# Fourteen of sixteen experts taken in order of token count, with a static row count for each place in the order

## The chip, the cores and the metric

The kernel runs on one core of a Trainium2 chip. The metric is device time in microseconds (us) of one launch, attention and mixture of experts together. The times in this document come from timed runs and from one profiled execution; stretches are given in us from the start of that execution's span.

## What is computed

A delta-rule attention over 768 steps (4 batches, 8 heads, head size 48) gives 3072 tokens of 384 features. A two-level gate then picks one of four groups and one of four experts in it for each token, and each token goes through its own expert alone: 384 to 1024 features, ReLU, and back to 384, times the two softmax weights.

```python
# x: (3072, 384), the attention's output, one row for each token
g_idx = np.argmax(x @ w_group, axis=1)
for g in range(4):
    mask_g = g_idx == g
    xg = x[mask_g]
    e_idx = np.argmax(xg @ w_expert[g], axis=1)
    for e in range(4):
        mask_e = e_idx == e
        h = np.maximum(xg[mask_e] @ w1[g, e], 0.0)
        ye = h @ w2[g, e]
        out[tok_idx] = (g_w * e_w)[:, None] * ye     # 0 for no token: each has one expert
```

How many tokens an expert gets depends on the data. For the inputs of this case (a fixed seed) the reference routes 203, 162, 176, 211, 203, 190, 203, 201, 181, 200, 183, 224, 195, 202, 155 and 183 tokens to experts 0 to 15. That is 3072 in all, 192 on average, and 224 at most.

## The kernel before

**Attention.** The tokens are worked through in 24 chunks of 32 steps. TensorE makes the products, VectorE inverts small triangular matrices (`inverse`), and ScalarE empties the accumulators. The order of these engines is written out by hand.

**Routing.** After each group of chunks `route` picks the expert of every token, and counts in `acc` how many tokens each expert has so far. Each expert owns a region of `room` rows in a DRAM buffer `x_dram`. A token's row number is the count before it (`slot_i`), and GpSimd writes the token there by an indirect DMA (L464), with its weight `cw` (L456, copied by L463) and its own number beside it. The regions' first 224 rows are zeroed at the start of the kernel (L177, 16 DMAs), so that rows with no token hold zeros. When all chunks are counted, a matmul with ones (L597) gives the totals of each expert, `last` (L598). From them L600 to L606 work out how many extra tiles of 128 tokens there are beyond the static 224 rows of each expert (`over`, its running sum `incl`, and the total `tot_i`).

**Experts.** The sixteen experts follow in their own order, 0 to 15, each with `SLOTS = 224` rows, in two halves of 112. TensorE, VectorE and ScalarE again run in the order in which the code is written; SyncE's queue, which issues the loads, is filled by the scheduler. For expert e:

- `take` (L616) reads its 224 rows from `x_dram` into `xg`, two experts ahead.
- `turn_in` (L625) transposes the rows, six transposes in all, and L627 copies them to `xt`.
- `hidden` (L636): 8 tiles of hidden features times 3 blocks of input features, each with a 128x128 block of `w1` as the stationary operand and the 224 rows as the moving one. Each product in 32-bit floats is two matmul records in the trace, so these are 48 records. ScalarE applies ReLU (L639).
- `second` (L650): 3 blocks of output features times 8 tiles, 48 records again. ScalarE copies (L652).
- `turn_out` (L661, L664, L665): six transposes, the product with the weight, and an indirect DMA from GpSimd that puts each row at its token's place in `out`. Rows with no token point beyond the end and are dropped.
- When `hidden` and `second` of expert e are done with their weights, the two buffers are reloaded with `w1` and `w2` of expert e + 2 (L122, 1536 KB each).

The halves of `turn_in` of the next expert lie between the parts of `second`, those of `turn_out` of the last expert between the parts of `hidden`. After the sixteen a loop of run-time length (L709) works through the extra tiles, `n_over` of them, one at a time. It reads the counts, loads the weights of that expert, takes 128 rows and sends them through the same steps with nothing beside it.

Of the kernel before, what the change touches and what calls it, by code (L numbers as in the profile page):

```python
# [8 lines left out]
F32 = mybir.dt.float32  # L9
I32 = mybir.dt.int32  # L10
# [8 lines left out]
SLOTS = 224  # L19
# [4 lines left out]
def constants(n_tokens, seq, n_experts, n_group, n_batch, room):  # L24
# [18 lines left out]
        "full": np.tile(first + SLOTS - 127, (128, 1)),  # L43
# [11 lines left out]
def deltanet_then_moe(  # L55
# [27 lines left out]
    T, P = 2, SLOTS // 2  # L83
    assert room % 32 == 0 and SLOTS % 32 == 0 and room >= N + 128
# [9 lines left out]
    x_dram = dp.tile([NE * room // 32, 32, XW], F32, name="x_dram")  # L94
# [7 lines left out]
    over = cp.tile([128, NE], F32, name="over")  # L102
    incl = cp.tile([128, NE], F32, name="incl")
# [11 lines left out]
    def load_expert(e, w1, w2, parts=1):  # L115
# [8 lines left out]
        return out  # L124

    weights = {}

    with ExitStack() as first:
# [31 lines left out]
        zero = ap_.tile([P, XW], F32, name="zero")  # L160
# [3 lines left out]
        def load_rest():  # L164
# [11 lines left out]
            for e in range(NE):  # L176
                nc.sync.dma_start(out=slots(e), in_=zero[:, None, :].to_broadcast([P, T, XW]))  # L177
# [196 lines left out]
        def route(r):  # L374
# [83 lines left out]
            for g, u in enumerate(us):  # L458
                x = xs.pop(u)
                if n == RG:  # L460
# [4 lines left out]
                    out=x_dram.rearrange("a b d -> (a b) d"),  # L465
# [132 lines left out]
        nc.vector.tensor_copy(last, n_ps)  # L598
        tiles_i = cp.tile([128, NE], I32, name="tiles_i")
        nc.vector.tensor_tensor(tiles_i, last, cut["full"], op=ALU.subtract)  # L600
# [74 lines left out]
    ready = {0: take(slots(0)), 1: take(slots(1))}  # L675
    xts, yts = {0: turned(ready[0][0])}, {}
    with tc.manual_schedule(engines={mybir.EngineType.PE, mybir.EngineType.DVE,
# [3 lines left out]
        for e in range(NE):  # L681
            if e + 2 < NE:
                ready[e + 2] = take(slots(e + 2))
# [25 lines left out]
    with tc.For_i(0, n_over):  # L709
        done = mp.tile([128, NE], F32, name="done")  # L710
# [6 lines left out]

        nc.vector.tensor_scalar(col, col, 4.0, float(SLOTS // 32), op0=ALU.mult, op1=ALU.add)
        nc.vector.scalar_tensor_tensor(col, in0=ef, scalar=float(room // 32), in1=col,
                                       op0=ALU.mult, op1=ALU.add)  # L720
# [8 lines left out]
                            max_val=NE * room // 32 - 4,  # L729
                            skip_runtime_bounds_check_because="a tile of the sorted tokens")  # L730
        end, lim = mp.tile([128, NE], F32, name="end"), mp.tile([128, 1], F32, name="lim")
        nc.vector.tensor_scalar(end, cut["expert"], ef, None, op0=ALU.is_equal)
# [72 lines left out]
```

## Time and profile before

| | us |
|---|---|
| median of 3 runs | 619.71 |
| lowest, highest | 618.38, 621.3 |
| the profiled execution, its own time | 617.58 |
| its span from the first to the last instruction | 615.8 |

| engine | busy us | share of the span |
|---|---|---|
| TensorE matmul (PE) | 517.1 | 84% |
| TensorE weight load (PEld) | 474.4 | 77% |
| VectorE (DVE) | 240.8 | 39% |
| ScalarE (ACT) | 175.7 | 29% |
| GpSimd (POOL) | 72.1 | 12% |

The shares are averages over two different stages, so they say little by themselves. Attention and routing end at about 280 us. The experts follow until about 601 us, and the last rows are written after that. A row of the trace names a line, an engine, an operation, the tiles that it writes and reads, its shapes and how often it ran. In a row of stages, the number after each engine is its busy time in that stretch; the granted clock is that of TensorE as a share of its full 2.4 GHz, so that 0.50 is 1.2 GHz.

### The profile page before, as it was taken

To read this page: it belongs to the slowest core of one execution; us is meant where nothing else is said; L and a number is where in the kernel's file an instruction comes from. 1 tells how busy PE (TensorE), PEld (TensorE's weight loads), DVE (VectorE), ACT (ScalarE), POOL (GpSimd) and SP (SyncE) were. 2 spreads that over 40 slices of the span, in tenths; PEclk is the share of its full clock that TensorE was granted. 3 is DMA by queue.
4 is the path that set the end of the run, shared out by engine and by line. 5 is a ranking of instruction groups with operands and counts; after the bars stand their busy time and mean duration, and the time that the engine had idled before them with its cause. 6 is when DMAs were issued, how large, how long until landed. Compare 5 with 4: busy or idle time off the path is not lost. (4 is left out here: it accounts for less than half of the span.)

```text
span 615.8 us, 18005 instructions
## 1 busy us (share of the span) xinstructions
PE 517.1 (84%) x8070; PEld 474.4 (77%) x8070; DVE 240.8 (39%) x738; ACT 175.7 (29%) x335; POOL 72.1 (12%) x130
## 2 busy tenths in 40 slices
PE   3305789979989788863999999999999999999990
PEld 2204667767767676752999999999999999999990
DVE  2698967989699894141011111011111111111000
ACT  2103245554655645430111111111111111111110
POOL 0100000003030132141011001110011000110011
PEclk9999679988979899985999999999999999999996
DMA  8996543425322132223255647555574655746000
GB/s 294 379 279 221 195 161 133 133 78 172 131 86 65 47 103 86 60 79 93 102 197 185 199 159 247 177 206 183 178 247 146 232 165 197 242 153 215 11 15 20
DMA packets 40351, 96.54 MB, mean 157 GB/s; under 512 B 3369, under 2 KB 24034, under 8 KB 40272
## 3 DMA queue, kind: packets, MB, share of 16 engines
q1 hardware_dynamic: 36688, 85.90, 42.2%
q0 software_dynamic: 3584, 9.47, 4.4%
q8 instruction: 64, 1.05, 0.7%
q14 instruction: 15, 0.12, 0.1%
HBM read 80.36 MB, written 15.78 MB: 156 GB/s over the span
## 5 line engine op out<-in xcount | busy, mean ns | idle before, releaser
L636 PE MATMUL h_ps<-xt,w 128*128 128x224 f32 x768 | 155.1, 356 | 0.6 <-DVE xt L627 0.6
L650 PE MATMUL y_ps<-hid,w 128*128 128x224 f32 x768 | 153.3, 353 | 0.0
L636 PEld LDWEIGHTS h_ps<-xt,w 128*128 128x128 f32 x768 | 144.7, 192 | 1.3 <-DVE xt L627 0.9
L650 PEld LDWEIGHTS y_ps<-hid,w 128*128 128x128 f32 x768 | 143.0, 190 | 0.0
L627 DVE COPY xt<-t_ps 128x336 f32<-128x336 f32 x32 | 16.2, 508 | 167.5 <-PE t_ps L625 167.5
L639 ACT ACTIVATE hid<-h_ps 128x448 f32<-128x448 f32 x64 | 34.8, 544 | 140.3 <-PE h_ps L636 140.3
L664 DVE TENSOR_SCALAR yo<-o_ps,xg 112x384 f32<-112x384 f32 x32 | 19.7, 617 | 120.4 <-PE o_ps L661 120.4
L665 POOL DMA_INDIRECT out_dram<-yo,at x32 | 30.1, 941 | 296.9 <-DVE yo L664 236.5
L264 DVE TENSOR_TENSOR m<-m,t 128x30 f32<-128x30 f32 (+9 forms) x180 | 59.5, 331 | 4.7
L260 DVE TENSOR_TENSOR t<-m 128x30 f32<-128x30 f32 (+9 forms) x180 | 59.4, 330 | 4.2
L297 PE MATMUL a_ps<-vh,con 128*128 128x384 f32 x48 | 26.9, 649 | 34.8 <-DVE vh L284 22.6
L652 ACT ACTIVATE yt<-y_ps 128x224 f32<-128x224 f32 x48 | 17.2, 357 | 134.3 <-PE y_ps L650 134.3
L335 ACT ACTIVATE s_bd<-s_ps 48x768 f32<-48x768 f32 x46 | 37.0, 804 | 17.3 <-PE s_ps L329 16.7
L297 PEld LDWEIGHTS a_ps<-vh,con 128*128 128x128 f32 x48 | 8.4, 218 | 37.8 <-DVE vh L284 19.8
L329 PE MATMUL s_ps<-w,kv 32*128 32x96 f32 x736 | 28.2, 292 | 4.7 <-ACT w L322 4.7
L303 PEld LDWEIGHTS a_ps<-s_bd,kqt 128*32 128x32 f32 x736 | 18.1, 125 | 15.9 <-issue 15.9
L319 PEld LDWEIGHTS w_ps<-f,mtb 64*64 64x64 f32 x768 | 25.4, 139 | 6.3 <-issue 4.0
L329 PEld LDWEIGHTS s_ps<-w,kv 32*128 32x128 f32 x736 | 24.3, 198 | 7.3 <-ACT w L322 5.7
L319 PE MATMUL w_ps<-f,mtb 64*64 64x48 f32 x768 | 28.4, 225 | 1.1 <-ACT f L307 1.1
L340 PE MATMUL o_ps<-w,gq 32*32 32x48 f32 x1536 | 24.2, 212 | 2.7 <-issue 2.7
L203 PE MATMUL g_ps<-kqt 48*32 48x64 f32 x1216 | 18.6, 249 | 7.8 <-DMA kqt<-in_kq_dram 4.1
L464 POOL DMA_INDIRECT x_dram<-x,slot_i x24 | 23.7, 986 | 8.7 <-POOL x L463 5.0
(95 smaller groups left out, 459.5 us busy)
## 6 DMA issues: line engine op xcount, KB each, us to landing
w<-in_w_dram SPq DMA_DIRECT2D x28, 1536.0 KB, 6.8
kqt<-in_kq_dram SPq DMA_DIRECT2D x24, 512.0 KB, 4.4
kv<-in_kv_dram SPq DMA_DIRECT2D x24, 448.0 KB, 3.9
x_dram<-zero SPq DMA_DIRECT2D x16, 337.8 KB, 9.4
xg<-x_dram SPq DMA_DIRECT2D x16, 337.8 KB, 3.2
w<-in_w_dram SPq DMA_DIRECT2D x6, 512.0 KB, 8.5
w<-in_w_dram SPq DMA_DIRECT2D x4, 576.0 KB, 7.7
w<-in_w_dram SPq DMA_DIRECT2D x2, 384.0 KB, 6.8
```

The lines of the kernel that those rows point to most:

```text
L260: nc.vector.tensor_tensor(tv, m[:, j + 1:, j:j + 1].to_broadcast([128, n, j]), m[:, j:j + 1, 0:j].to_broadcast([128, n, j]), op=ALU.mult)
L264: nc.vector.tensor_tensor(m[:, j + 1:, 0:j], m[:, j + 1:, 0:j], tv, op=ALU.add)
L297: nc.tensor.matmul(a_ps.rearrange("p h d -> p (h d)"), lhsT=ident, rhs=vh.rearrange("p h d -> p (h d)"), start=True, stop=(u == 0), skip_g ...
L319: nc.tensor.matmul(w_ps[b, h], lhsT=mt[b, uu * H + (h % 2) * NP + h // 2], rhs=f[b, h], start=True, stop=True, skip_group_check=True)
L329: nc.tensor.matmul(s_at[:, b, j], lhsT=k[quads[b], j], rhs=w[quads[b], 2 * j:2 * j + 2], start=(u == 0 and j == 0), stop=True, skip_group_ ...
L335: nc.scalar.activation(s_bd[rows, :, :, hh, :], s_at[rows, :, :, hh * D:(hh + 1) * D], ACT.Copy)
L340: nc.tensor.matmul(o_ps[b, h], lhsT=gq[b, (h % 2) * NP + h // 2], rhs=w[b, h], start=(u == 0 and h == 0), stop=True, skip_group_check=True)
L464: put = nc.gpsimd.indirect_dma_start(out=x_dram.rearrange("a b d -> (a b) d"), out_offset=bass.IndirectOffsetOnAxis(ap=slot_i[:, g], axis= ...
L636: nc.tensor.matmul(h_ps[:, k], lhsT=w1[:, j, (f + k) * 128:(f + k + 1) * 128], rhs=xt[:, j], start=(j == 0), stop=(j == DC - 1), skip_grou ...
L639: nc.scalar.activation(hid[:, f:f + 2], h_ps, ACT.Relu)
L650: nc.tensor.matmul(y_ps, lhsT=w2[:, f, j * 128:(j + 1) * 128], rhs=hid[:, f], start=(f == 0), stop=(f == FC - 1))
L665: nc.gpsimd.indirect_dma_start(out=out[:, :], out_offset=bass.IndirectOffsetOnAxis(ap=at[:, i:i + 1], axis=0), in_=yo[:, :], in_offset=Non ...
```

## The change

The experts 0 and 1 (`FIXED = 2`) stay first, with 224 static rows each. The other fourteen are sorted by their token count, the largest first, on the chip, once the totals are known. Place k of that order has its own static number of rows: 232, 220, 214, 208, 204, 202, 200, 196, 192, 188, 184, 182, 176 and 168. The loop over sixteen experts is then a loop over places, and which expert stands at a place is read from the table `order_i` into a register of SyncE (L718 of the changed kernel), which addresses the rows in `x_dram` and the two weight matrices. `slots_of` keeps for each expert the static rows that it got, for the count of extra tiles and for the loop over them.

The sort makes a 16x16 table of comparisons, sums it into a rank, compares the rank with 0 to 15, and sums twice more, for `order` and for `slots_of`. The tables are 256 elements wide on each partition. The constants grow by 32 columns, and the zeroed part of each region from 224 to 232 rows. In the loop over extra tiles the row arithmetic is in rows and no longer in blocks of 32; it is left out of the diff here.

```diff
-SLOTS = 224
+FIXED = 2
+SLOTS = [224] * FIXED + [232, 220, 214, 208, 204, 202, 200, 196, 192, 188, 184, 182, 176, 168]
...
-    def slots(e):
-        rows = x_dram[e * room // 32:(e * room + SLOTS) // 32].rearrange("a b d -> (a b) d")
-        return rows.rearrange("(p t) d -> p t d", t=T)
+    def slots(e, n):
+        return x_dram[e, 0:n].rearrange("(o p t) d -> p (o t) d", o=1, t=T)
...
+    def load_any(ev, w1, w2):
+        for t, d in ((w1, w1_d), (w2, w2_d)):
+            nc.sync.dma_start(out=t, in_=d[ds(ev, 1)].rearrange("o (c p) f -> p (o c) f", p=128))
...
-                nc.sync.dma_start(out=slots(e), in_=zero[:, None, :].to_broadcast([P, T, XW]))
+                nc.sync.dma_start(out=slots(e, max(SLOTS)),
+                                  in_=zero[:, None, :].to_broadcast([max(SLOTS) // T, T, XW]))
...
         nc.vector.tensor_copy(last, n_ps)
+        key = cp.tile([128, NE], F32, name="key")
+        nc.vector.scalar_tensor_tensor(key, in0=last, scalar=16.0, in1=cut["tie"], op0=ALU.mult,
+                                       op1=ALU.add)
+        table, rank = cp.tile([128, NE, NE], F32, name="table"), cp.tile([128, NE], F32, name="rank")
+        like = [128, NE, NE]
+        nc.vector.tensor_tensor(table, key[:, None, :].to_broadcast(like),
+                                key[:, :, None].to_broadcast(like), op=ALU.is_gt)
+        nc.vector.tensor_reduce(rank, table, axis=AX.X, op=ALU.add)
+        nc.vector.tensor_tensor(table, rank[:, None, :].to_broadcast(like),
+                                cut["expert"][:, :, None].to_broadcast(like), op=ALU.is_equal)
...
+        nc.vector.tensor_tensor(picked, table, cut["expert"][:, None, :].to_broadcast(like),
+                                op=ALU.mult)
+        nc.vector.tensor_reduce(order, picked, axis=AX.X, op=ALU.add)
+        nc.vector.tensor_copy(order_i, order)
+        nc.vector.tensor_tensor(picked.rearrange("p e k -> p k e"), table,
+                                cut["slots"][:, :, None].to_broadcast(like), op=ALU.mult)
+        nc.vector.tensor_reduce(slots_of, picked, axis=AX.X, op=ALU.add)
         tiles_i = cp.tile([128, NE], I32, name="tiles_i")
-        nc.vector.tensor_tensor(tiles_i, last, cut["full"], op=ALU.subtract)
+        nc.vector.tensor_tensor(last, last, cut["first_all"], op=ALU.subtract)
+        nc.vector.scalar_tensor_tensor(tiles_i, in0=last, scalar=127.0, in1=slots_of, op0=ALU.add,
+                                       op1=ALU.subtract)
...
-    ready = {0: take(slots(0)), 1: take(slots(1))}
+    ready = {e: take(slots(e, SLOTS[e])) for e in range(FIXED)}
...
             if e + 2 < NE:
-                ready[e + 2] = take(slots(e + 2))
+                ev = nc.values_load(order_i[0:1, e + 2:e + 3], engines=[mybir.EngineType.SP],
+                                    min_val=0, max_val=NE - 1,
+                                    skip_runtime_bounds_check_because="an index of one of NE")
+                ready[e + 2] = take(x_dram[ds(ev, 1), 0:SLOTS[e + 2]].rearrange(
+                    "o (p t) d -> p (o t) d", t=T))
...
             if e + 2 < NE:
                 weights[e + 2] = expert_tiles(e + 2)
-                for piece in load_expert(e + 2, *weights[e + 2]):
-                    piece()
+                load_any(ev, *weights[e + 2])
```

On VectorE the place that moves is the end of routing, where the last group's weights `cw` and the totals are worked out side by side. Before, `last` is followed by the last group's route (`slot_i`, `ed`, `gd`, `cw`), with the small steps on `tiles_i` and `over` in between:

```order
L598 COPY last<-n_ps 128x16
L440 TENSOR_REDUCE slot_i_4964<-rk_4963 128x2
L444 TENSOR_REDUCE ed_4968<-sx_4942 128x8
L446 TENSOR_REDUCE gd_4967<-sx_4942 128x2
L600 TENSOR_TENSOR tiles_i<-last,con 128x16
L448 SCALAR_TENSOR_TENSOR ed_4968<-ed_4968,gh_4938 128x8
L601 TENSOR_SCALAR tiles_i<-tiles_i 128x16
L451 TENSOR_REDUCE cw_4969<-ed_4968 128x2
L602 CAST over<-tiles_i 128x16
L453 SCALAR_TENSOR_TENSOR cw_4969<-gd_4967,cw_4969 128x2
L603 TENSOR_SCALAR over<-over 128x16
L456 RECIPROCAL cw_4969<-cw_4969 128x2
```

In the changed kernel the same stretch, behind the copy to `last` (L610), reads as follows (the output of `rank` is 16 wide, what it reads is 256 wide):

```order
L452 TENSOR_REDUCE slot_i_4965<-rk_4964 128x2
L456 TENSOR_REDUCE ed_4969<-sx_4943 128x8
L458 TENSOR_REDUCE gd_4968<-sx_4943 128x2
L614 SCALAR_TENSOR_TENSOR key<-last,con 128x16
L460 SCALAR_TENSOR_TENSOR ed_4969<-ed_4969,gh_4939 128x8
L618 TENSOR_TENSOR table<-key 128x256
L463 TENSOR_REDUCE cw_4970<-ed_4969 128x2
L633 TENSOR_TENSOR last<-last,con 128x16
L620 TENSOR_REDUCE rank<-table 128x16
L465 SCALAR_TENSOR_TENSOR cw_4970<-gd_4968,cw_4970 128x2
L621 TENSOR_TENSOR table<-rank,con 128x256
L468 RECIPROCAL cw_4970<-cw_4970 128x2
```

Ahead of the reciprocal that ends `cw` there now stand three steps that are 256 wide; the rest of the sort and the count of extra tiles come after it.

On SyncE's queue the place is the loads of the first experts. Before, the rows of three experts are taken in one go, and then come the weights of expert 2:

```order
L616 DMA xg<-x_dram 112x772 x3
L122 DMA w_2_5100<-in_w_dram 128x3x1024
L122 DMA w_2_5101<-in_w_dram 128x8x384
L616 DMA xg<-x_dram 112x772
L122 DMA w_3_5201<-in_w_dram 128x3x1024
L122 DMA w_3_5202<-in_w_dram 128x8x384
```

After it, the register is loaded once for each place, and each DMA that it addresses has an instruction ahead of it that sets the address (ISA):

```order
L651 DMA xg<-x_dram 112x772 x2
L718 TENSOR_LOAD order_i
L651 ISA
L651 DMA xg<-x_dram 116x772
L135 ISA
L135 DMA w_2_5120<-in_w_dram 128x3x1024
L135 ISA
L135 DMA w_2_5121<-in_w_dram 128x8x384
L718 TENSOR_LOAD order_i
```

The two fixed experts' rows stay ahead of the first register load; everything for the other fourteen stands behind it.

## Rows read from the trace of the kernel before

**Rows 1.** Busy time of each engine in stages; clock, DMA share, GB/s last.

```profile
core 0: us, PE busy (x) PEld busy (x) DVE busy (x) ACT busy (x) POOL busy (x), PEclk, DMA share, GB/s
20.00:50.00 30.00, 4.39 (x227) 3.45 (x226) 23.40 (x69) 1.83 (x3) 1.05 (x6) 1.00 1.06 325
...
270.00:285.70 15.70, 2.98 (x17) 2.48 (x16) 4.81 (x38) 1.46 (x5) 7.08 (x13) 0.58 0.39 133
285.70:293.00 7.30, 6.00 (x18) 4.94 (x19) 1.09 (x3) 0.00 (x0) 0.00 (x0) 0.50 0.17 47
...
300.00:400.00 100.00, 100.00 (x557) 98.97 (x556) 11.62 (x25) 16.78 (x36) 9.45 (x10) 1.00 0.58 194
```

**Rows 2.** Timeline of TensorE, experts 0 and 1: start us, us, instructions in a row.

```profile
299.94 3.19 PE L650 MATMUL y_ps<-hid,w 128*128 128x224 f32 x16
302.97 0.45 PE L625 MATMUL t_ps<-con,xg 112*128 112x112 f32 x3
...
319.37 3.19 PE L650 MATMUL y_ps<-hid,w 128*128 128x224 f32 x16
```

**Rows 3.** Instructions of one line: count, duration in ns (min/median/max).

```profile
L636 PE MATMUL h_ps<-xt,w x48: 352/352/355, 406.8 to 416.3; 128*128 128x224 f32 x48
L297 PE MATMUL a_ps<-vh,con x48: 486/590/1009, 51.8 to 263.9; 128*128 128x384 f32 x48
L369 PEld LDWEIGHTS l_ps<-wr,xt x144: 186/192/333, 73.6 to 272.3; 128*128 128x128 f32 x144
```

**Rows 4.** Timeline of weight loads ahead of 20- and 64-column matmuls.

```profile
263.17 0.30 PEld L432 LDWEIGHTS r_ps<-acc,con 128*128 128x128 f32 x2
...
267.97 0.74 PEld L369 LDWEIGHTS l_ps<-wr,xt 128*128 128x128 f32 x6 [0.71 <-ACT w L322]
```

**Rows 5.** The page's costliest groups: what runs beside the expert matmuls.

```profile
L627 DVE COPY xt<-t_ps 128x336 f32<-128x336 f32 x32 | 16.2, 508 | 167.5 <-PE t_ps L625 167.5
L639 ACT ACTIVATE hid<-h_ps 128x448 f32<-128x448 f32 x64 | 34.8, 544 | 140.3 <-PE h_ps L636 140.3
L664 DVE TENSOR_SCALAR yo<-o_ps,xg 112x384 f32<-112x384 f32 x32 | 19.7, 617 | 120.4 <-PE o_ps L661 120.4
L665 POOL DMA_INDIRECT out_dram<-yo,at x32 | 30.1, 941 | 296.9 <-DVE yo L664 236.5
```

**Rows 6.** Timeline from the totals to the first expert's matmuls; waits in brackets.

```profile
275.92 0.17 DVE L598 COPY last<-n_ps 128x16 f32<-128x16 f32 x1 [0.21 <-PE n_ps L597]
...
277.09 0.16 DVE L456 RECIPROCAL cw<-cw 128x2 f32<-128x2 f32 x1
...
277.31 0.18 POOL L463 COPY x<-cw 128x1 f32<-128x1 f32 x1 [1.41 <-DVE cw L456]
...
282.37 1.28 SPq L616 DMA_DIRECT2D xg<-x_dram  x3
...
285.80 0.79 PE L625 MATMUL t_ps<-con,xg 112*128 112x112 f32 x3 [9.92 <-DMA xg<-x_dram]
...
288.62 11.49 PE L636 MATMUL h_ps<-xt,w 128*128 128x224 f32 x48 [0.60 <-DVE xt L627]
```

**Rows 7.** Timeline of VectorE in the attention stage: 256- and 198-wide steps, one after another.

```profile
30.50 0.41 DVE L211 TENSOR_TENSOR gq<-g_ps,con 128x256 f32<-128x256 f32 x1
30.83 0.35 DVE L260 TENSOR_TENSOR t<-m 128x198 f32<-128x198 f32 x1
```

**Rows 8.** The same view as rows 3: a register load on SyncE's queue.

```profile
L707 SPq TENSOR_LOAD <-tot_i x1: 488/488/488, 562.8 to 562.8; - x1
```

**Rows 9.** What SyncE's queue waited for, 280 to 616 us: total, times, longest.

```profile
SPq L122 <- PE y_ps L650: 129.4, 14, 9.3
SPq L122 <- PE h_ps L636: 61.8, 14, 16.5
```

**Rows 10.** DMA issues: count, KB each, median us from issue to landing.

```profile
w<-in_w_dram SPq DMA_DIRECT2D x28, 1536.0 KB, 6.8
...
x_dram<-zero SPq DMA_DIRECT2D x16, 337.8 KB, 9.4
xg<-x_dram SPq DMA_DIRECT2D x16, 337.8 KB, 3.2
```

More of the change, by code (lines that the diff above doesn't have):

```diff
@@ L42, in constants @@
         "first": (p[:, None] == 0) * first[None, :],
-        "full": np.tile(first + SLOTS - 127, (128, 1)),
+        "first_all": np.tile(first, (128, 1)),
+        "tie": np.tile(n_experts - 1 - np.arange(n_experts) - 16 * first
+                       + (1 << 20) * (np.arange(n_experts) < FIXED), (128, 1)),
+        "slots": np.tile(SLOTS, (128, 1)),
         "expert": np.tile(np.arange(n_experts), (128, 1)),
@@ L82, in deltanet_then_moe @@
     NS = N // 128
-    T, P = 2, SLOTS // 2
-    assert room % 32 == 0 and SLOTS % 32 == 0 and room >= N + 128
+    T = 2
+    assert room >= N + 128 and len(SLOTS) == NE == 16 and not any(n % T for n in SLOTS)
     assert B * C == 128 and NCH % RG == 0
@@ L709, in deltanet_then_moe @@
     with tc.For_i(0, n_over):
-        done = mp.tile([128, NE], F32, name="done")
+        done, end, here = [mp.tile([128, NE], F32, name=n) for n in ("done", "end", "here")]
+        lim = mp.tile([128, 1], F32, name="lim")
         nc.vector.tensor_scalar(done, incl, taken, None, op0=ALU.is_le)
@@ L716, in deltanet_then_moe @@
         nc.vector.tensor_tensor(col, taken, col, op=ALU.subtract)
-        nc.vector.tensor_scalar(col, col, 4.0, float(SLOTS // 32), op0=ALU.mult, op1=ALU.add)
-        nc.vector.scalar_tensor_tensor(col, in0=ef, scalar=float(room // 32), in1=col,
-                                       op0=ALU.mult, op1=ALU.add)
+        nc.vector.tensor_scalar(end, cut["expert"], ef, None, op0=ALU.is_equal)
+        nc.vector.tensor_tensor(here, end, slots_of, op=ALU.mult)
+        nc.vector.tensor_reduce(lim, here, axis=AX.X, op=ALU.add)
+        nc.vector.scalar_tensor_tensor(col, in0=col, scalar=128.0, in1=lim, op0=ALU.mult,
+                                       op1=ALU.add)
+        nc.vector.scalar_tensor_tensor(col, in0=ef, scalar=float(room), in1=col, op0=ALU.mult,
+                                       op1=ALU.add)
         pick = mp.tile([128, 2], I32, name="pick")
@@ L728, in deltanet_then_moe @@
         cv = nc.values_load(pick[0:1, 1:2], engines=[mybir.EngineType.SP], min_val=0,
[L729 removed]
+                            max_val=NE * room - 128,
                             skip_runtime_bounds_check_because="a tile of the sorted tokens")
[L731 to L732 removed]
         nc.vector.tensor_tensor(end, end, last, op=ALU.mult)
         nc.vector.tensor_reduce(lim, end, axis=AX.X, op=ALU.add)
+        nc.vector.scalar_tensor_tensor(lim, in0=ef, scalar=float(room), in1=lim, op0=ALU.mult,
+                                       op1=ALU.add)
         row, used = mp.tile([128, 1], F32, name="row"), mp.tile([128, 1], F32, name="used")
[L736 to L737 removed]
+        nc.vector.tensor_tensor(row, col, cut["part"], op=ALU.add)
         nc.vector.tensor_tensor(used, row, lim, op=ALU.is_lt)
```

23 lines of the change are left out of this document (11 added, 12 removed).

## The prediction

> **What bounds the kernel now.** I read the stages first, since the shares of the whole span mix two kinds of work. From 300 to 400 us TensorE is busy for all of 100 us, at the full 2.4 GHz, while VectorE, ScalarE and GpSimd are busy 12, 17 and 9 us of it [rows 1]; the stretches to 600 us read the same. So the expert stage is a stream of matmul records with no gap, and whatever shortens the records shortens the kernel. The timeline gives the size of one record: 16 records of `second` start at 299.94, and what follows them starts at 302.97, so 3.03 / 16 = 189.4 ns from start to start [rows 2]. The same place one expert later is at 319.37: a period of 19.43 us. It is made of 96 records x 189.4 ns = 18.18 us, and 1.25 us for the 12 transposes.
>
> The question for the forecast is what the 189.4 ns are made of: the 224 rows that stream through, or the 128x128 weight block that is loaded for each record. Weight loads are busy 98.97 of the same 100 us [rows 1], so the busy shares can't tell these apart. The durations can. A record with 224 columns lasts 352 ns and one with 384 columns, behind the same kind of 128x128 block, 486 ns at its shortest [rows 3]: 134 ns for 160 columns, **0.8375 ns a column**, about two cycles at 2.4 GHz. The load by itself is seen where little streams: six loads ahead of 20-column matmuls take 0.74 us [rows 4], the last of them 192 ns [rows 3], so (0.74 - 0.19) / 5 = 110 ns from start to start; the two ahead of 64-column ones take 0.30 us, again 110 ns apart [rows 4]. A load's own record of 192 ns is thus mostly latency, overlapped by the next one. From 20 to 64 columns nothing changes, so this is a floor; the line 189.4 - 0.8375 x (224 - n) comes down to it at n = 129. All places of the new order, 168 to 232, lie above.
>
> **The change part by part.** *Rows.* The fourteen sorted places have 2766 rows in all, against 14 x 224 = 3136: 370 fewer. Each row is one column in 96 records, so 370 x 96 x 0.8375 ns = **29.75 us** less. Upper bound: all of the record proportional to columns, 189.4 / 224 = 0.8455 ns, or 30.0 us. Lower bound: the chord from 64 columns (110 ns) to 224, 79.4 / 160 = 0.496 ns, or 17.6 us. I take the slope between 224 and 384, since the flat piece from 20 to 64 speaks for a floor and a line rather than a chord. If the floor in this stream stood at 160 ns, well above what the rows show, the five shortest places would lose 3.7 us of the gain; that goes into the range.
>
> [...]
>
> *Transposes.* Each expert has 12, 104 ns each (1.25 us / 12). Half of them stream half of the expert's rows, the other half load them as weights. In proportion, that is at most 6 x 185 x 0.8375 ns = 0.9 us less, and nothing if they are held by the fixed side. I take 0.4.
>
> *The sort on VectorE.* The path from routing to the first expert is a chain with nothing beside it: `cw` ends at L456, GpSimd waited for it, scatters two chunks, SyncE reads the rows at 282.37, and TensorE, which waited 9.92 us for them, starts [rows 6]. The order of the changed kernel puts three 256-wide steps (L618, L620, L621) and two small ones where four small ones stood, between `last` and `cw`, 1.17 us apart before (275.92 to 277.09) [rows 6]. A 256-wide step holds the next one back by 0.33 us where they don't depend on each other [rows 7], a small one by about 0.11 (1.17 us in 11 steps). So 3 x 0.33 - 2 x 0.11 = **0.8 us** more, all on the path: GpSimd, SyncE and TensorE move by as much. If every wide step is waited for to its end, 0.41 us, 1.1; if the routing steps fill in better, 0.6. The remaining wide steps and small ones, some 3 us, run while the scatters (5 us) are on their way, so `order_i` is ready before SyncE asks for it. Were that cover gone, it would delay only the third expert's rows, which are not needed until 40 us later.
>
> *SyncE.* Fourteen register loads at 0.49 us each [rows 8], and an address instruction ahead of each of 42 DMAs, of a kind that no run here times; 0.1 to 0.5 us each by the register load as its nearest row, at most 2 us for each expert. Queued behind them are the rows (3.2 us to land) and weights (6.8 us) of the expert two places on [rows 10]. SyncE does nothing else then: its weight loads waited for TensorE 14 times for `hidden` and 14 times for `second`, up to 16.5 us at a time [rows 9]. Weights that are ordered when a buffer falls free are needed a period and a half later, 22 us even at 168 rows. Cost nothing; cover 13 us.
>
> *What else takes turns.* At 168 rows a pair of tiles in `hidden` takes 12 x 142 ns = 1.7 us, against 544 ns for its ReLU; copies and products take 0.5 to 0.6, and GpSimd 2 x 0.94 us, in a period of 14.9 [rows 5]. Nothing there becomes late.
>
> *Zeroes and constants.* 16 x 8 rows more, 0.2 MB at 325 GB/s [rows 1], is 0.6 us of transfer early on. Zeroes have 9.4 us to land [rows 10] and are not read until 282 us; what stands behind them in the queue is weights of the experts 0 and 1. I take 0; 0.6 is the upper end.
>
> *The clock.* The first expert runs at 1.2 GHz until 293.0 [rows 1], 4.4 us from its start [rows 6], after TensorE had been nearly idle for 15 us. That stretch costs half of itself, and it may come out a little longer or shorter: +-1 us, sum 0.
>
> **Sum.** 617.58 - 29.75 - 0.4 + 0.8 = 588.2 us against the profiled execution, which is 2.1 us under the median of the runs. Against the median 619.71 - 29.35 = **590.4 us**, which I give.
>
> **Rivals.** *The weight load is the bound.* If each record waits for its own 128x128 block for 189 ns, columns are free, and the time is 619.71 - 0.4 + 0.8 = 620.1. For it: weight loads are busy 99% of the stage. Against it: they come 110 ns apart where columns are few. The Trainium skill's page "Perfetto Trace Analysis", section Identifying the Most-Contended Engine, names busy weight loads as the better measure of how near TensorE is to its limit; by that reading there is no headroom here, but the 110 ns say that the busy time is waiting. Chance 3%.
>
> *Load and stream stand one behind the other.* Then 110 of the 189.4 ns are the load and 79.4 the stream, 0.354 ns a column, and the rows bring 12.6 us: 607.5. For it: the sum fits at 224 columns as well. Against it: 64 columns cost no more than 20, and 384 add 0.8375 ns each. [...] Chance 2%.
>
> *A place is too small.* This is the case on the slower side, and that in which the change doesn't do what it says. By the reference's counts, sorted, the places have 8, 9, 11, 5, 2, 1, 0, 1, 2, 5, 1, 1, 0 and 13 rows to spare; one token more on a place with none to spare, or a sort that is off by one, gives a pass of the loop over extra tiles. Its price, one step after another: VectorE's row arithmetic about 3 us, a register load 0.5, rows or weights about 9 (6.8 us for a weight, or zeroes' scatter and 3.2 for the rows), transposes 1.4, 96 records at the floor of 110 ns or at half the clock, 10.5 to 21, and the way out 5: 29 to 40 us, so 625 with 35. It decides from one token. Against it: the counts fit, 32 of L627 are 16 x 2 [rows 5], so no expert had more than 224 before, and the nearest tie of two gate scores in the reference is 7e-6 on a scale of 0.016. Chance 3%.
>
> *The weights come late.* If rows and both weights of an expert landed one after another, 3.2 + 2 x 6.8 = 16.8 us, the five shortest places, with periods of 14.9 to 16.5 us, would wait 4.7 us in all: 595. Against it: the period and a half above, and 194 GB/s in this stage where 325 were moved earlier [rows 1]. Chance 3%.
>
> **How the numbers follow.** 89% for the forecast. Low end, against the profiled execution: 617.6 - 30.0 - 0.9 + 0.6 - 1 = 586. High end, against the median: 590.4 plus 3.7 (floor at 160 ns), 0.6 (zeroes), 0.3 (sort) and 1 (clock): 596, which takes in the late weights. The three other rivals, and the chord's 602, are left out. A measurement of this kernel can tell about 0.5%, 3.1 us, from no change. Faster: 89 + 3 + 2 = 94%; same 3%; slower 3%.
>
> **What would show it.** In the profile after: records of L636 and L650 (other line numbers) with 168 columns some 142 ns apart, periods falling from 20.1 to 14.9 us, TensorE still without a gap; `cw` 0.8 us later behind `last`, and the first row read as much later; no copy to `xt` (L627) beyond 32; SyncE's weight loads waiting for TensorE. Gaps ahead of the transposes or of L636 would mean late loads, records that stay at 189 ns the first rival, and a tail beyond the last scatter the second.

## The result, and the profile after

The changed kernel takes 600.09 us (median of 4 runs, 599.31 to 600.61) where the kernel before takes 619.05 us beside it (4 runs, 617.45 to 621.3): a ratio of 0.969, 95% interval 0.966 to 0.972. The direction is as forecast; the gain is 19 us where 29 were expected, and the time lies above the range. The profiled execution went from 617.58 to 600.61 us, its span from 615.8 to 598.8. Cut at four points that both traces have, the span moved like this:

| stretch | before | after | difference |
|---|---|---|---|
| start to the copy of the totals into `last` | 275.92 | 291.70 | **+15.8** |
| from there to the first expert's first matmul | 12.70 | 14.19 | +1.5 |
| first to last expert matmul | 313.1 | 282.6 | **-30.5** |
| behind the last matmul | 14.05 | 10.3 | -3.75 |
| sum | 615.8 | 598.8 | -17.0 |

The expert stage did what was forecast. What was lost was lost in the attention stage, 200 us ahead of the first sorted expert.

**The expert stage.** TensorE's timeline at the last place of the order (start us, us, instructions in a row), which answers [rows 2]:

```profile
580.46 7.00 PE L685 MATMUL y_ps<-hid,w 128*128 128x168 f32 x48
...
587.30 0.38 PE L696 MATMUL o_ps<-con,yt 128*84 128x128 f32 x2
...
587.86 0.64 PE L696 MATMUL o_ps<-con,yt 128*84 128x128 f32 x4 [0.18 <-ACT yt L687]
```

The last of these rows ends the expert stage, at 588.50 us; in the kernel before it is this one:

```profile
601.10 0.65 PE L661 MATMUL o_ps<-con,yt 128*112 128x128 f32 x4 [0.23 <-ACT yt L652]
```

48 records in 6.84 us are 142.5 ns from start to start, where 224 columns took 189.4 [rows 2]. The durations by shape answer [rows 3] (busy us, mean ns of one behind the bar):

```profile
L685 PE MATMUL y_ps<-hid,w 128*128 128x232 f32 x48 | 9.9, 360 | 0.0
...
L685 PE MATMUL y_ps<-hid,w 128*128 128x168 f32 x48 | 7.0, 306 | 0.0
```

That is 54 ns for 64 columns, 0.84 ns a column. And by stage, in the columns of [rows 1], here with two stretches of the attention stage:

```profile
30.00:40.00 10.00, 1.17 (x64) 0.96 (x64) 9.31 (x26) 0.00 (x0) 0.00 (x0) 1.00 0.28 91
90.00:100.00 10.00, 0.00 (x0) 0.00 (x0) 0.00 (x0) 0.00 (x0) 0.00 (x0) 0.50 1.02 386
400.00:500.00 100.00, 100.00 (x616) 99.34 (x615) 13.21 (x29) 17.42 (x40) 15.20 (x10) 1.00 0.65 209
```

From 400 to 500 us TensorE has no gap, as in [rows 1], at more records in the same time. The other two rows are the loss. From 90 to 100 us no engine does anything. From 30 to 40 us all three busy engines read as before, but the DMA engines move 91 GB/s at a busy share of 0.28. The same stretch of the kernel before:

```profile
30.00:40.00 10.00, 1.17 (x64) 0.96 (x64) 9.31 (x25) 0.00 (x0) 0.00 (x0) 1.00 1.07 299
```

**Where the loss begins.** SyncE's queue from 19 us on, in the changed kernel:

```profile
19.58 59.06 SPq L188 DMA_DIRECT2D x_dram<-zero  x16
78.68 8.74 SPq L129 DMA_DIRECT2D w<-in_w_dram  x6
87.53 3.49 SPq L154 DMA_DIRECT2D kqt<-in_kq_dram  x1
91.14 0.37 SPq L157 DMA_DIRECT2D kv<-in_kv_dram  x1
```

and in the kernel before:

```profile
19.89 18.59 SPq L177 DMA_DIRECT2D x_dram<-zero  x16
38.61 7.65 SPq L122 DMA_DIRECT2D w<-in_w_dram  x6
46.87 1.09 SPq L143 DMA_DIRECT2D kqt<-in_kq_dram  x1
59.62 0.34 SPq L146 DMA_DIRECT2D kv<-in_kv_dram  x1
```

The sixteen stores of zeroes hold the queue for 59 us instead of 19, for 3.6% more bytes; one store takes 3.7 us (median) to issue, one later load 0.33. Behind them stand not only expert weights but the reloads of the attention's own inputs, `kqt` and `kv`: the `kv` that was ordered at 59.6 us is now ordered at 91.1. VectorE's timeline, with the wait in brackets:

```profile
100.77 0.56 DVE L296 TENSOR_TENSOR vh<-kv,normt 128x384 f32<-128x384 f32 x1 [17.77 <-DMA kv<-in_kv_dram]
```

and its waits for `kv` from 50 to 280 us (total, times, longest):

```profile
DVE vh L296 <- DMA kv<-in_kv_dram: 22.9, 3, 17.8
```

The step that waits builds `vh`, from which the products of a chunk start, so everything behind it comes later. The kernel before has no wait for `kv` in that list. The late order is not the whole of the wait: from its order to the step that reads it `kv` takes 9.6 us here (91.14 to 100.77), where the kernel before has a median of 3.9 us from order to landing. The queue released six pieces of expert weights and a `kqt` just ahead of it, and the DMA engines are full from 90 to 100 us (1.02, 386 GB/s).

The 15.8 us are not that wait alone either. At the fifth `vh` the changed kernel is 21.7 us behind (107.04 against 85.34), at the sixth 14.3 us (114.39 against 100.09). Between the two the kernel before lost time of its own: its granted clock was 0.50 from 85 to 90 us.

**From the totals to the first expert**, the rows that answer [rows 6]:

```profile
291.70 0.17 DVE L610 COPY last<-n_ps 128x16 f32<-128x16 f32 x1 [0.21 <-PE n_ps L609]
...
293.65 0.16 DVE L468 RECIPROCAL cw<-cw 128x2 f32<-128x2 f32 x1
293.88 0.36 POOL L475 COPY x<-cw 128x1 f32<-128x1 f32 x1 [2.20 <-DVE cw L468]
...
299.30 1.88 SPq L651 DMA_DIRECT2D xg<-x_dram  x3
...
303.07 0.79 PE L660 MATMUL t_ps<-con,xg 112*128 112x112 f32 x3 [11.41 <-DMA xg<-x_dram]
...
305.89 11.13 PE L671 MATMUL h_ps<-xt,w 128*128 128x224 f32 x48 [0.60 <-DVE xt L662]
```

`cw` follows `last` by 1.95 us, against 1.17: the 0.8 us of the sort. The rest of the +1.5 lies in the DMAs behind it: 0.34 us from the row read to the first transpose (3.77 against 3.43 us), the other 0.4 between GpSimd's copy and SyncE's read, where the scatters land. In the versions below with 240, 234 and 256 rows zeroed this whole stretch is 13.4 to 13.6 us long, 0.7 to 0.9 more than before, so the DMAs' part does not come back there.

**SyncE beside the experts**, its waits from 280 us on, in the columns of [rows 9], and one line's durations in the view of [rows 8] (count, ns min/median/max):

```profile
SPq L135 <- PE y_ps L685: 115.7, 14, 9.4
...
SPq L135 <- PE h_ps L671: 53.7, 14, 15.7
...
L718 SPq TENSOR_LOAD <-order_i x14: 273/466/570, 300.2 to 542.0; - x14
```

The loads still wait for TensorE 14 and 14 times, and TensorE waits for none of them.

**The tail.** GpSimd's drains at the end of the program (ns min/median/max), after and then before:

```profile
L840 POOLq DRAIN  x3: 40/103/980, 597.0 to 598.6; - x3
```

```profile
L801 POOLq DRAIN  x3: 40/103/4655, 610.3 to 615.5; - x3
```

3.7 us less in one drain is the whole difference in the tail.

### The profile page after: what moved, and what is told of

It reads as the page before. It is cut to its first block, busy times and chain, and to the rows that moved or that the text cites. A ratio compares the mean times of both kernels' runs of the same rounds, so it can differ in the third digit from the quotient of the medians.

```text
span 598.8 us, 18113 instructions
## 1 busy us (share of the span) xinstructions
PE 483.8 (81%) x8070; PEld 442.2 (74%) x8070; DVE 243.7 (41%) x748; ACT 172.0 (29%) x335; POOL 81.7 (14%) x130
## 5 line engine op out<-in xcount | busy, mean ns | idle before, releaser
L671 PE MATMUL h_ps<-xt,w 128*128 128x224 f32 (+14 forms) x768 | 140.0, 336 | 0.6 <-DVE xt L662 0.6
L685 PE MATMUL y_ps<-hid,w 128*128 128x224 f32 (+14 forms) x768 | 138.8, 334 | 0.0
L671 PEld LDWEIGHTS h_ps<-xt,w 128*128 128x128 f32 x768 | 130.9, 192 | 1.5 <-DVE xt L662 0.9
L685 PEld LDWEIGHTS y_ps<-hid,w 128*128 128x128 f32 x768 | 129.3, 190 | 0.3
L662 DVE COPY xt<-t_ps 128x336 f32<-128x336 f32 (+14 forms) x32 | 15.1, 472 | 149.9 <-PE t_ps L660 149.9
L700 POOL DMA_INDIRECT out_dram<-yo,at x32 | 38.5, 1203 | 258.8 <-DVE yo L699 117.5
L674 ACT ACTIVATE hid<-h_ps 128x448 f32<-128x448 f32 (+14 forms) x64 | 32.4, 506 | 128.8 <-PE h_ps L671 128.8
L699 DVE TENSOR_SCALAR yo<-o_ps,xg 112x384 f32<-112x384 f32 (+14 forms) x32 | 19.6, 616 | 106.2 <-PE o_ps L696 106.2
L276 DVE TENSOR_TENSOR m<-m,t 128x30 f32<-128x30 f32 (+9 forms) x180 | 59.6, 331 | 4.7
L687 ACT ACTIVATE yt<-y_ps 128x224 f32<-128x224 f32 (+14 forms) x48 | 16.2, 339 | 120.2 <-PE y_ps L685 120.2
L215 PE MATMUL g_ps<-kqt 48*32 48x64 f32 x1216 | 18.6, 247 | 8.8 <-issue 4.8
L288 ACT ACTIVATE mtb<-mt,con 128x1024 f32<-128x1024 f32 x12 | 13.0, 1134 | 41.4 <-DVE mt L283 41.4
```

The lines of the kernel that those rows point to most:

```text
L276: nc.vector.tensor_tensor(m[:, j + 1:, 0:j], m[:, j + 1:, 0:j], tv, op=ALU.add)
L671: nc.tensor.matmul(h_ps[:, k], lhsT=w1[:, j, (f + k) * 128:(f + k + 1) * 128], rhs=xt[:, j], start=(j == 0), stop=(j == DC - 1), skip_grou ...
L674: nc.scalar.activation(hid[:, f:f + 2], h_ps, ACT.Relu)
L685: nc.tensor.matmul(y_ps, lhsT=w2[:, f, j * 128:(j + 1) * 128], rhs=hid[:, f], start=(f == 0), stop=(f == FC - 1))
L699: nc.vector.tensor_scalar(yo, o_ps, xg[:, i, DM:DM + 1], None, op0=ALU.mult)
L700: nc.gpsimd.indirect_dma_start(out=out[:, :], out_offset=bass.IndirectOffsetOnAxis(ap=at[:, i:i + 1], axis=0), in_=yo[:, :], in_offset=Non ...
```

## The experiments

Two theories were set against each other first. One: the stores are slow because of their shape, 232 rows from 116 partitions. The other: the new layout of `x_dram`, the larger region or something else in the change makes the stores slow or the attention late, and the shape has no part in it. Later runs ask what about the 116 it is, whether the queue or the transfer does the harm, and what the sort itself costs. Times are medians, ratios are against the kernel before, measured beside each.

**The kernel before, zeroed as the changed kernel zeroes** (nothing else of the change):

```diff
-        zero = ap_.tile([P, XW], F32, name="zero")
+        zero = ap_.tile([116, XW], F32, name="zero")
...
-                nc.sync.dma_start(out=slots(e), in_=zero[:, None, :].to_broadcast([P, T, XW]))
+                rows = x_dram[e * room // 32:(e * room + 256) // 32].rearrange("a b d -> (a b) d")
+                nc.sync.dma_start(out=rows[0:232].rearrange("(p t) d -> p t d", t=T),
+                                  in_=zero[:, None, :].to_broadcast([116, T, XW]))
```

> The kernel before, with 232 instead of 224 rows of each region zeroed, from 116 partitions; nothing else is changed. Theory A: the 16 stores take about 59 us, VectorE waits for kv, and the time grows by about 16 us, from 619 to 635. Theory B: 0.6 us more, 619 to 620, since only 0.2 MB is added.

It takes 635.65 us, ratio 1.026 (1.018 to 1.033), 17.0 us slower than the kernel before (618.67); by the interval 11 to 21. Its queue, and then VectorE's waits, in the views above:

```profile
20.06 59.09 SPq L178 DMA_DIRECT2D x_dram<-zero  x16
```

```profile
DVE vh L286 <- DMA kv<-in_kv_dram: 23.6, 3, 18.3
```

That is a loss of the same size, made in a kernel without the sort, the larger constants, the new order or the new layout of `x_dram`. None of them is needed for it.

**The changed kernel with the old store and the last rows apart:** sixteen stores of 224 rows from 112 partitions, and one for the last 8 rows of all regions.

```diff
-                nc.sync.dma_start(out=slots(e, max(SLOTS)),
-                                  in_=zero[:, None, :].to_broadcast([max(SLOTS) // T, T, XW]))
+                nc.sync.dma_start(out=slots(e, 224), in_=zero[0:112, None, :].to_broadcast([112, T, XW]))
+            nc.sync.dma_start(out=x_dram[:, 224:max(SLOTS)],
+                              in_=zero[0:NE, None, :].to_broadcast([NE, max(SLOTS) - 224, XW]))
```

> The changed kernel, with the same 232 rows of each region zeroed in another cut: 16 stores of 224 rows from 112 partitions, as before the change, and one more store for the last 8 rows of all regions. Theory A (a store from 116 partitions is carried by few of the 16 DMA engines, 0.28 of them busy, so the 16 stores take 59 us instead of 19, hold up SyncE's queue, and VectorE waits 17.8 us for the reload of kv behind them): the stores are issued in about 20 us, the wait for kv is gone, and the time falls from 600 to about 584 us. Theory B (the new layout of x_dram or the larger region makes the stores slow, or the attention is late for another reason): no change, 600 us.

586.67 us, ratio 0.945 (0.939 to 0.951). The sixteen stores are back at 19.7 us, with the same 232 rows zeroed, and the sort, the constants, the order and the layout as in the changed kernel:

```profile
19.30 19.70 SPq L188 DMA_DIRECT2D x_dram<-zero  x16
```

**More rows, other partition counts.** Four kernels zero 256, 240, 234 and 238 rows of each region, from 128, 120, 117 and 119 partitions. They differ from the changed kernel in these lines alone (here with 120):

```diff
-        zero = ap_.tile([max(SLOTS) // T, XW], F32, name="zero")
+        zero = ap_.tile([120, XW], F32, name="zero")
...
-                nc.sync.dma_start(out=slots(e, max(SLOTS)),
-                                  in_=zero[:, None, :].to_broadcast([max(SLOTS) // T, T, XW]))
+                nc.sync.dma_start(out=slots(e, 240),
+                                  in_=zero[:, None, :].to_broadcast([120, T, XW]))
```

> The changed kernel, with 256 rows of each region zeroed, from 128 partitions: 10% more bytes than in the changed kernel. Theory A: 128 partitions spread over all DMA engines again, the stores take about 19 x 256 / 224 = 21 us, and the time is about 585 us. If bytes or the number of rows were the cause: over 600 us.

> The changed kernel, with 240 rows of each region zeroed, from 120 partitions. Theory A says that what counts is how the number of partitions divides among 16 engines: 116 is 4 x 29, 120 is 8 x 15, 112 and 128 are multiples of 16. So 8 engines work here, the stores take about 35 to 40 us, and the queue is free at about 65 us, before the reload of kv is needed: 585 to 588 us. If only multiples of 16 are fast and all else is as slow as 116: 600 us.

> The changed kernel, with 234 rows of each region zeroed, from 117 partitions = 9 x 13. My rule of multiples fell with 120 partitions, which were as fast as 128. Rule C (the store is cut into as many equal parts as the largest divisor of the partition count up to 16: 4 for 116, 15 for 120, 13 for 117): the 16 stores take about 20 x 15 / 13 = 23 us, DMA engines 0.8 busy, and the time is 583 to 586 us. Rule D (the number of rows must be a multiple of 16, as 224, 240 and 256 are): as slow as 232 rows, 59 us and 600 us.

> The changed kernel, with 238 rows of each region zeroed, from 119 partitions = 7 x 17. Rule C: 7 engines, 0.44 busy, the 16 stores take 59 x 4 / 7 x 238 / 232 = 35 us, the queue is free at about 64 us, and the time is 583 to 587 us, since the reloads behind it are needed later than that. Rule D: 59 us and 600 us.

Their stores in SyncE's queue, in the order 128, 120, 117, 119 partitions:

```profile
19.62 20.68 SPq L188 DMA_DIRECT2D x_dram<-zero  x16
```

```profile
19.21 20.04 SPq L188 DMA_DIRECT2D x_dram<-zero  x16
```

```profile
21.35 22.09 SPq L188 DMA_DIRECT2D x_dram<-zero  x16
```

```profile
22.01 33.32 SPq L188 DMA_DIRECT2D x_dram<-zero  x16
```

| partitions | largest divisor up to 16 | stores hold the queue, us | time, us | ratio (interval) |
|---|---|---|---|---|
| 112 (and one store more) | 16 | 19.7 | 586.67 | 0.945 (0.939 to 0.951) |
| 116 (the changed kernel) | 4 | 59.06 | 600.09 | 0.969 (0.966 to 0.972) |
| 117 | 13 | 22.09 | 583.16 | 0.943 (0.937 to 0.949) |
| 119 | 7 | 33.32 | 590.0 | 0.954 (0.948 to 0.960) |
| 120 | 15 | 20.04 | 583.09 | 0.943 (0.937 to 0.950) |
| 128 | 16 | 20.68 | 584.29 | 0.944 (0.938 to 0.950) |

So neither the bytes nor "a multiple of 16" decide: 256 rows cost no more than 224, and 117 partitions are as good as 120. The largest divisor of the partition count up to 16 sets the 4, the 7 and the 13 apart from the rest, in that order; 15 and 16 (19.7 to 20.7 us for 224 to 256 rows) are not told apart. That rule came out of the 120: a multiple of 8 and not of 16, it was expected at half the rate and ran at the full one. The runs with 117 and 119 were then its test. 35 us were expected of the 119, and it took 33.3. The share of busy DMA engines, with 119 partitions:

```profile
30.00:40.00 10.00, 1.17 (x64) 0.96 (x64) 9.31 (x25) 0.00 (x0) 0.00 (x0) 1.00 0.47 158
```

In the same ten us the kernel before reads 1.07 and the changed kernel 0.28, as shown above. If 1.07 stands for all 16, 0.47 is 7.0 engines and 0.28 is 4.2.

The Trainium skill, page "DMA: Bandwidth & Descriptors", section Why a DMA increments its semaphore by 16 and not by 1, states this rule: a DMA uses the largest number of engines up to 16 that divides the outermost dimension of both sides. All six rows are in line with it. It bore on the step of the prediction that failed, and the prediction did not weigh it.

The time of the 119 is not explained by its stores: 583 to 587 us were expected. VectorE waits only 1.3 us for `kv` there, as with 120, yet the time is 7 us above the 117 and the 120. The granted clock is the likeliest reason. To the fifth `vh` the profiles of the 119 and the 117 stay within 0.6 us (85.14 and 84.59), at the sixth they are 6.3 us apart (102.34 and 96.07). Between 85 and 95 us TensorE was granted 0.77 and then 0.55 of its clock in the 119 and all of it in the 117, and no engine waits for a DMA there. The timed runs say the same. The 112-partition version took 591.66, 587.33, 586.01 and 583.49 us in runs with a mean clock of 0.943, 0.949, 0.949 and 0.966; the 119 took 590.46 and 589.55 us at 0.946 and 0.947.

**The same slow store on another queue:** one word of the changed kernel.

```diff
-                nc.sync.dma_start(out=slots(e, max(SLOTS)),
+                nc.gpsimd.dma_start(out=slots(e, max(SLOTS)),
```

> The changed kernel with its sixteen zero stores (232 rows from 116 partitions, as in the changed kernel) ordered by GpSimd's queue instead of SyncE's. Theory (the slow store hurts by what stands behind it in SyncE's queue: weights, kqt, kv): the stores still move about 91 GB/s and need 59 us or so on their own queue, but kv is there in time, VectorE's wait for kv falls from 17.8 us to under 4, and the time falls from 600 to 583 to 590. Rival (a store that keeps a few DMA engines busy slows whatever shares them, in any queue): kv still comes 10 us late or more, and the time stays at 595 to 602. Third (GpSimd's own first work is behind the stores): GpSimd is late with its first constants and the time lies between.

This run and the one with the last place at 224 rows, below, came from a chip on which the kernel before took 639.14 us, so their ratios are read and not their times. The ratio is 0.957 (0.947 to 0.967): better than the changed kernel's 0.969, short of the 0.943 of the good shapes. The first theory was right that `kv` is there in time: VectorE has no wait for it. Its 59 us were wrong, and so was the premise of the second. From 20 to 50 us the DMA engines are busy, in the columns of the windows above:

```profile
20.00:50.00 30.00, 6.38 (x320) 4.78 (x311) 18.12 (x49) 2.41 (x4) 7.98 (x13) 1.00 0.96 271
```

A share of 0.96 and 271 GB/s: from GpSimd's queue the same 116 partitions are not slow at all. So the handful of engines comes with this store on SyncE's queue, and not with the count alone. (The section of the Trainium skill cited above names an exception to its rule, some direct copies from GpSimd that use all sixteen; this run agrees with it.) What this kernel pays is something else. GpSimd starts its stores at 1.5 us, in the middle of the attention's first loads, and SyncE's own loads then crawl. Its four loads of `kqt` hold the queue for 13 us, against 4.0 with 240 rows, and the products `g_ps` on TensorE wait 9.3 us in all for `kqt` in the first 110 us, against 4.2. The queue, and VectorE's first `vh`:

```profile
31.86 12.97 SPq L154 DMA_DIRECT2D kqt<-in_kq_dram  x4
...
59.59 0.53 DVE L296 TENSOR_TENSOR vh<-kv,normt 128x384 f32<-128x384 f32 x1
```

That first `vh` is at 51.87 us in the version with 240 rows, 7.7 us earlier. The third theory named the time, between the two, but not this reason: GpSimd's own first step on `acc` is late (36.45 us against 18.07), and no engine waits for GpSimd in the first 110 us. So this kernel shows two prices. A store on few engines blocks what stands behind it on its queue, and a store on all engines, this early, delays the loads that run beside it.

**The sort behind the route** (with 240 rows zeroed): the sort's steps are moved behind the last group's route in the order written by hand, so that nothing wide stands ahead of `cw`. The lines are the same, one level deeper in the code.

```diff
-        n_ps = ps.tile([128, NE], F32, tag="s", name="n_ps")
-        nc.tensor.matmul(n_ps, lhsT=ones, rhs=acc[:, NCH], start=True, stop=True)
-        nc.vector.tensor_copy(last, n_ps)
...
+            n_ps = ps.tile([128, NE], F32, tag="s", name="n_ps")
+            nc.tensor.matmul(n_ps, lhsT=ones, rhs=acc[:, NCH], start=True, stop=True)
+            nc.vector.tensor_copy(last, n_ps)
...
```

> The kernel with 240 rows zeroed from 120 partitions, and the sort written into the hand-set order behind the last group's route, so that none of its steps stands between the totals and the weights cw. If the sort's wide steps are what makes cw late: from the product rk to the end of cw it takes 1.2 us instead of 2.4, as in the group before, and the first read of rows comes 1.2 us earlier relative to rk; the time is 1.2 us lower, which only the profile can show. If GpSimd or the scatters hold the path: cw is earlier and the first read isn't.

VectorE from the last group's rank `rk` to `cw`, with 240 rows and the sort as in the change:

```profile
272.44 0.19 DVE L449 TENSOR_TENSOR rk<-r_ps,hot 128x32 f32<-128x32 f32 x1 [0.80 <-PE r_ps L444]
...
274.80 0.16 DVE L468 RECIPROCAL cw<-cw 128x2 f32<-128x2 f32 x1
```

and with the sort behind it:

```profile
276.56 0.19 DVE L449 TENSOR_TENSOR rk<-r_ps,hot 128x32 f32<-128x32 f32 x1 [0.80 <-PE r_ps L444]
...
277.69 0.17 DVE L468 RECIPROCAL cw<-cw 128x2 f32<-128x2 f32 x1
```

2.36 us became 1.13, and SyncE's first row read follows `rk` by 6.6 us instead of 7.8. The 1.2 us are there in the trace. In the time, 583.91 us, ratio 0.944 (0.939 to 0.948), they can't be told from the 583.09.

**All places at 224 rows** (with 240 rows zeroed): the sort and the addressing at run time stay, the saving in rows goes.

```diff
-SLOTS = [224] * FIXED + [232, 220, 214, 208, 204, 202, 200, 196, 192, 188, 184, 182, 176, 168]
+SLOTS = [224] * FIXED + [224] * 14
```

> The kernel with 240 rows zeroed, the sort and the run-time expert numbers, but 224 rows at each of the fourteen places: 370 rows more. If the gain is the rows alone and everything else (register loads, address instructions, weights by run-time number) is hidden: 370 x 96 x 0.8375 ns + 0.4 = 30 us more than with the static counts, so about 613 us, and TensorE without gaps in the expert stage. If the run-time addressing cost or gained something by itself, the expert stage would differ from the kernel before, 313.1 us from its first matmul to its last.

621.0 us, ratio 1.002 (0.998 to 1.005), 8 us more than expected. Its expert stage, first to last matmul, takes 312.5 us, against 313.1 before and 282.2 (286.31 to 568.53) with the changed places: the places are worth 30.3 us, as expected, and a table of experts read at run time costs nothing while nothing waits for SyncE. The 8 us lie at both ends. One part is the tail, 3.9 us longer: the drain is back at its old length.

```profile
L840 POOLq DRAIN  x3: 40/103/4655, 616.0 to 621.2; - x3
```

The other is the attention stage, whose copy to `last` is at 281.12 us, against 272.84 with 240 rows and the changed places, though nothing in that stage differs. These 8.3 us are the extreme: the profiled executions are the slowest of ten runs and the fastest of four, 42.7 us apart where the medians are 37.9. The windows from 100 to 250 us of the one and of the other (granted clock third from the end):

```profile
100.00:250.00 150.00, 131.66 (x4055) 107.01 (x4043) 124.42 (x401) 82.72 (x146) 25.57 (x58) 0.92 0.30 98
```

```profile
100.00:250.00 150.00, 130.27 (x4231) 106.65 (x4230) 124.00 (x406) 85.67 (x152) 29.65 (x69) 0.97 0.33 105
```

TensorE was granted 0.92 of its full clock in one and 0.97 in the other. Over the kernels without a late `kv`, the copy to `last` follows that clock:

| kernel | clock, 100 to 250 us | copy to `last`, us |
|---|---|---|
| 240 rows zeroed | 0.97 | 272.84 |
| 117 partitions | 0.93 | 274.63 |
| before | 0.94 | 275.92 |
| 128 partitions | 0.94 | 276.24 |
| sort behind the route (the copy itself is moved back by 0.8 us) | 0.94 | 277.77 |
| all places at 224 | 0.92 | 281.12 |
| 119 partitions | 0.92 | 282.08 |
| 112 partitions and one store | 0.90 | 283.60 |

That is a spread of 11 us in one stage, with the clock in the same order but for the 117 partitions. The run with the last place at 224 rows, below, carries it on, on its other chip: 0.85 and 302.20 us. This is seen, not shown: no run here sets the clock. It is enough to say that single profiles of these kernels differ by several us ahead of the experts without any cause in the code, and that the six ratios in the table above can't be told apart where they differ by under 1%.

**The last place at 224 rows** (with 240 rows zeroed): does the drain go by the last scatters' row count?

```diff
-SLOTS = [224] * FIXED + [232, 220, 214, 208, 204, 202, 200, 196, 192, 188, 184, 182, 176, 168]
+SLOTS = [224] * FIXED + [232, 220, 214, 208, 204, 202, 200, 196, 192, 188, 184, 182, 176, 224]
```

> The version that zeroes 240 rows, with the last place of the order at 224 rows instead of 168. Its 56 rows more are 56 x 96 x 0.8375 ns = 4.5 us of expert stage. Theory (the drain at GpSimd's end goes by the row count of the last scatters): the drain at the end reads 4655 ns again where 168 rows gave 980, the tail behind the last matmul is 14 us instead of 10.3, and the time is 583.1 + 4.5 + 3.7 = 591.3. Rival (the drain goes by all the scatters of the stage, or by chance): the drain stays near 1 us, and the time is 587.6.

Ratio 0.956 (0.949 to 0.962). Times the 618.7 us that the kernel before takes elsewhere this is 591, what the theory gives, but the interval, 587 to 595 us, holds the rival's 587.6 as well. The time does not decide, the trace does:

```profile
L840 POOLq DRAIN  x3: 40/103/980, 612.1 to 613.6; - x3
```

The drain stayed at 980 ns, so the theory fell; the tail is 10.4 us. What the traces show is that the drain is 4655 ns in the three kernels whose scatters of expert rows all come from 112 partitions (before, before with the 116-partition zeroes, all places at 224). It is 898 to 980 in all that mix partition counts, whichever comes last. Why is left open.

## Why the prediction was wrong, step by step

*The step that failed* is the one on zeroes: "I take 0; 0.6 is the upper end". It measured 15.8 us in the trace, 17.0 us in the kernel before with nothing but that store changed, and 0.026 of 619 us, 16 us, between the changed kernel and the one with 240 rows. Two things in it were wrong. The rate, 325 GB/s, was that of a store from 112 partitions, taken over to one from 116 as if only the size had changed; it fell to 91. And the sentence "what stands behind them in the queue is weights of the experts 0 and 1" left out `kqt` and `kv`, which the queue's rows show at 46.87 and 59.62 us of the kernel before. "Not read until 282 us" was true of the zeroes and beside the point: what counts is when the queue is free again. In place of nothing the runs show a queue held until 78.7 us, and VectorE waiting 17.8 us for a `kv` that was ordered 31.5 us later than before. No rival held this mechanism, and so the range, whose upper end took 0.6 us for it, could not hold the time.

*Rows and transposes*, -29.75 and -0.4: measured -30.5 from first to last matmul. The two terms make -30.15; the other 0.36 is the first `hidden`, 11.13 us against 11.49 [rows 6]: it ran at a granted clock of 0.50 for some 3.7 us (0.61 on average from 308 to 310 us) instead of 4.4. The slope is 0.84 ns a column between 232 and 168 columns, against 0.8375, and the spacing at 168 columns is 142.5 ns, against 142. The floor lies below 168, as argued. This settles two rivals: with the weight load as the bound, and with load and stream one behind the other, the stage would have lost nothing or 12.6 us. Weight loads are still busy 99.34 of 100 us in a stream whose records at the last place take 25% less time, so that share was no bound.

*The sort*, +0.8: `cw` came 0.78 us later, as worked out, and moving the sort took 1.2 us out. The path to the first matmul grew by 1.5 in this profile, since the scatters and the row read, taken as unchanged, took 0.7 us longer; with 240, 234 and 256 rows it grew by 0.7 to 0.9.

*SyncE*: right. Register loads took 466 ns (median), the address instructions 37 and 29 ns ahead of each DMA, and nothing on TensorE waited. So the weights did not come late; nor was a place too small, since the copy to `xt` (L662) ran 32 times.

*What else takes turns*: right for TensorE, though it had a near miss that the prediction did not see. GpSimd's scatter of expert rows, before in the first fence and after in the second (count, ns min/median/max):

```profile
L665 POOL DMA_INDIRECT out_dram<-yo,at x32: 937/942/958, 313.3 to 606.5; - x32
```

```profile
L700 POOL DMA_INDIRECT out_dram<-yo,at x32: 933/1007/2301, 330.2 to 593.4; - x32
```

Four of them took 2.2 to 2.3 us, both at the place of 107 partitions and both at that of 101. The first of each:

```profile
407.36 2.30 POOL L700 DMA_INDIRECT out_dram<-yo,at  x1 [12.73 <-DVE yo L699]
...
460.86 2.22 POOL L700 DMA_INDIRECT out_dram<-yo,at  x1 [5.87 <-DVE yo L699]
```

Both counts are prime. The other places line up by the same largest divisor up to 16 as the stores: 1.48 us at 94 partitions (divisor 2), 1.18 and 1.26 at 92 and 116 (4), 1.08 at 102 (6), and 0.93 to 1.02 where it is 10 or more. The traces with 240 and 256 rows repeat this within 0.02 us; no run was made to test it. The longest scatter now takes 13.5 us to land (5.5 before). In the middle of the stage there is time for that. At the last place it would lie on the end; no run shows that.

*The clock*, +-1: enough for the first expert, the only stretch that it looked at (-0.36 us), but too narrow for the kernel. From 100 to 250 us the clock was the same in these two profiles, 0.94 and 0.93, but over all kernels it goes with 11 us of the attention stage.

*Not in the sum*: the 3.7 us of the drain, in favour of the change. With the zeroes put right, the kernels come to 583 to 584 us (117, 120, 128 partitions), 6 to 7 us under the forecast. 3.7 of it is this drain, and about 1 is that the kernel before took 618.7 to 619.0 us beside them and not the 619.71 from which the forecast starts. The other 1 to 3 us are not traced: the attention stage of their profiles ends at 274.63, 272.84 and 276.24 us, on either side of the 275.92 before.

The version that beats both kernels is the change with 240 rows zeroed from 120 partitions: 583.09 us, ratio 0.943 (0.937 to 0.950).

## What to carry to other kernels

When a change alters a DMA's partition count, price the DMA anew: look at the largest divisor up to 16 of the new count before taking over the old rate, and pad the count where that is small, since padding was free here (20.0 us for 240 rows, 19.7 for 224). Then read the whole queue behind it, not only the consumer of its data, and ask who waits for each entry. And a term that is set to zero deserves its own rival: what would the time be if its rate fell by four?

## What the runs showed of the hardware that was not expected

- On SyncE's queue the store ran at 91 GB/s from 116 partitions, and sixteen of them took 59 us, against 18.6 to 22 us from 112, 117, 120 and 128, and 33 us from 119. From GpSimd's queue the same 116 partitions kept the DMA engines 0.96 busy.
- GpSimd's row scatter from 107 or 101 partitions took 2.2 to 2.3 us of the engine instead of 0.94 us, and 1.2 to 1.5 us from 92, 94 or 116.
- GpSimd's drain at the end of the program took 4655 ns where all expert-row scatters had 112 partitions, and 898 to 980 ns where they were mixed.
- With the same code in the attention stage, the granted clock from 100 to 250 us ranged from 0.90 to 0.97 over the profiles of the table, and the copy to `last` from 283.6 to 272.8 us.
